# Keys and values of a token tile in three matmul groups instead of four, in a gated linear-attention kernel

## The chip, the cores and the metric

The kernel runs on one core of a Trainium2 chip. Time is device time in microseconds (us) of one execution, the median over several runs. The profile comes from one execution. Its engines are PE (TensorE, the matmuls), PEld (weight loads of TensorE), DVE (VectorE), ACT (ScalarE), POOL (GpSimd) and SP (SyncE, which issues most DMAs). "L92" is line 92 of the kernel.

## The reference

x has 2048 tokens of D = 576 columns, and all data are float32.

```python
xn = _layernorm(x)
# s: linear attention, 32 heads of 18 columns
q, k, v = heads of (xn @ wqkv)
pq, pk = q @ w_phi, k @ w_phi                        # per head
phi_q = concat(softmax(pq), softmax(-pq))            # per head, and phi_k from pk
kv = phi_k^T v;  z = sum of phi_k over tokens
s = ((phi_q kv) / (phi_q z + 1e-6)) @ wo
# g: a feed-forward layer of width 4608
g = silu((silu(xn @ w_gate) * (xn @ w_up)) @ w_down)
return x + s * g
```

## The kernel before

The work runs in four stages. The **preparation** (lines 137 to 254, about 0 to 71 us of the profile) normalizes the tokens, transposes them into the tiles X (`XB`), and lays out the weights. The **key/value loop** (lines 347 to 378, about 71 to 227 us) goes over 16 tiles of 128 tokens and sums phi_k^T v into `kvp`. The **query loop** (lines 431 to 496, to about 493 us) forms q, the numerators and the projection by `wo`. Then the **feed-forward** part runs to the end. Some of its matmuls are taken out as "early tiles" (line 110, tile `pe`), which have lower priority than the attention and fill TensorE where that has nothing ready.

Every float32 product is taken as a sum of products of rounded parts: operands are split into a high part (type fp32r) and a low part, and `xw` (line 82) adds up 14 matmuls for one output: for each half of the 576 rows, two chunks with three products each, and a 96-row chunk in which the parts are stacked. The tokens' tile is the stationary operand, and the weights stream past, so the number of columns of the output is the width of each matmul.

The weights of keys and values lie side by side in `KVWH` and `KVWL` (1152 columns): 576 for the keys, into which `w_phi` has been folded (`fold`, line 210, call at line 234), then 576 for the values, split from six loaded chunks at lines 242 to 249 by ACT, POOL and DVE. The six loads and the five of the query weights (line 252) share five buffers (`wst`).

In the key/value loop a token tile goes through these steps, in program order:

- lines 350 to 353: two groups of 14 matmuls of 288 columns for the keys, into the two PSUM banks of `pk` (tag `p2`, one buffer);
- lines 354 to 356, and `softmax_parts` (line 268): on DVE per head max, subtraction, min, subtraction, all four reading `pk`; two exponentials on ACT; then sum, reciprocal and multiplication on DVE, which give `phi`;
- lines 358 to 369: two groups of 14 matmuls of 288 columns for the values, each into a one-bank tile `pv` (tag `p`, one buffer), and copies of them on ACT into `v`, in which the 576 columns lie in five groups of seven heads (GW = 126 columns, the last 72) with a column of ones each;
- lines 370 to 371, between the two value groups: `kv_step` (line 286) of the tile before, ten matmuls of phi against v;
- lines 372 to 377: `background` (line 325), small steps that form sums of X for the feed-forward part on POOL, ACT and DVE (lines 305 to 323), and store them by DMA.

The order of instructions on each engine is fixed when the program is built: a planner takes instructions by priority (program order, raised where the code says `high_priority`) and by its own estimate of when their operands and buffers are ready. On the chip each engine follows its list and waits for semaphores. A tile with one buffer can be written again only when all readers of its last contents are done. PSUM has eight banks of 512 float32 columns; in the loop three hold `kvp`, two `pk`, one `pv`, and two the early tiles. In the profile both `p` and `p2` appear as `p`, since buffer numbers are left out.

Of the kernel before, what the change touches and what calls it, by code (L numbers as in the profile page):

```python
# [9 lines left out]
F32 = mybir.dt.float32  # L10
# [6 lines left out]
S, D, H, DH, F = 2048, 576, 32, 18, 4608  # L17
P = 128
# [5 lines left out]
HALF = D // 2  # L24
GH = 7
GW = GH * DH
# [11 lines left out]
def heads(ap):  # L38
    return ap.rearrange("p (h d) -> p h d", d=DH)


def spread(ap, n):
    return ap.unsqueeze(2).to_broadcast([P, n, DH])
# [3 lines left out]
def gated_hedgehog_kernel(ctx: ExitStack, tc, x, w_qk, w_v, w_phi, wo, w_gu, w_tail, w_down, ident_in, mask_in, out):  # L47
# [5 lines left out]
    nc = tc.nc  # L53
# [28 lines left out]
    def xw(ps, i, j, cols, wh, wl, stationary_x):  # L82
        pairs = []
        for k in range(2):
            b = XB[i][2 * j + k]
            for c in range(2):
                pairs += [(b[:, c, cols], w[:, k, c]) for w in (wh, wl)]
                pairs += [(b[:, 3 + c, cols], wh[:, k, c])]
            pairs += [(b[0:96, 2, cols], wh[0:96, k, 2])]
        for n, (a, b) in enumerate(pairs):  # L90
            l, r = (a, b) if stationary_x else (b, a)
            nc.tensor.matmul(ps, l, r, start=n == 0, stop=n == len(pairs) - 1)  # L92
# [30 lines left out]
    with ExitStack() as att:  # L123
# [8 lines left out]
        with ExitStack() as kst:  # L132
            kw = kst.enter_context(tc.tile_pool(name="kw", bufs=1))
            KVWH = kw.tile([P, 2, 3, 2 * D], F32R, name="KVWH")
            KVWL = kw.tile([P, 2, 2, 2 * D], F32R, name="KVWL")

            with ExitStack() as pst:
# [72 lines left out]
                def fold(ws, hi, lo):  # L210
                    for g, (o, w) in enumerate(GROUPS):
                        ps = pps.tile([P, 2, BT], F32, name="tp", bufs=3)
                        po = ps[:, :, 0:3 * P].rearrange("p a (c n) -> p a c n", c=3)
                        for k in range(2):
                            for c in range(3):
                                o2 = (3 * k + c) * P
                                nc.tensor.matmul(po[:, k, c, 0:w], ws[g][0:w, o2:o2 + P],
                                                 PHI[0:w, g].rearrange("p h f -> p (h f)")[:, 0:w],
                                                 start=True, stop=True)
                        split_rows(hi[:, :, :, o:o + w], lo[:, :, :, o:o + w], po[:, :, :, 0:w])  # L220
# [6 lines left out]
                wk = load_fold(0)  # L227
# [3 lines left out]
                first_weights = [early_weights(0)]  # L231
                with tc.issue_after(chain.ins):
                    norm_stats([3], xns[4:8])
                fold(wk, KVWH[:, :, :, 0:D], KVWL[:, :, :, 0:D])
                norm_block(3, xns[4:8])
                first_weights.append(early_weights(1))
                wv = []
# [3 lines left out]
                xns = load_x(0) + load_x(1)  # L241
                for n in range(6):
                    k, c = divmod(n, 3)
                    src, vh = wv[n][:, 0:D], KVWH[:, k, c, D:2 * D]
                    nc.scalar.copy(vh, src)
                    if c < 2:
                        nc.gpsimd.tensor_sub(KVWL[:, k, c, D:2 * D], src, vh)
                    else:
                        nc.vector.tensor_sub(vh[64:96], src[64:96], vh[64:96])
                wq = load_fold(1)  # L250
                norm_stats([0, 1], xns)
                norm_block(0, xns[0:4])
# [7 lines left out]
            kk = kst.enter_context(tc.tile_pool(name="kk", bufs=2))  # L260
            kps = kst.enter_context(tc.tile_pool(name="kps", bufs=1, space=PSUM))
# [5 lines left out]

            def softmax_parts(ps, e):
                m = kk_pool.tile([P, 2, H], F32, name="m")
                p4 = ps[:, :, 0:HALF].rearrange("p a (h d) -> p a h d", d=DH)  # L270
                for s, op in enumerate((ALU.max, ALU.min)):
                    m3 = m[:, s].rearrange("p (a h) -> p a h", a=2)
                    nc.vector.tensor_reduce(m3, p4, axis=AX.X, op=op)
                    nc.vector.tensor_sub(e[:, s * D:(s + 1) * D].rearrange("p (a h d) -> p a h d", a=2, d=DH), p4,  # L274
                                         m3.unsqueeze(3).to_broadcast([P, 2, H // 2, DH]))
                for s in range(2):
                    nc.scalar.activation(e[:, s * D:(s + 1) * D], e[:, s * D:(s + 1) * D], AF.Exp,
                                         scale=1.0 if s == 0 else -1.0)
                sm = kk_pool.tile([P, 2 * H], F32, name="sm")
                nc.vector.reduce_sum(sm, heads(e), axis=AX.X)  # L280
                nc.vector.reciprocal(sm, sm)
                return sm
# [3 lines left out]
            def kv_step(n, phi, v):  # L286
                for i in range(2 * NG):
                    g, s = divmod(i, 2)
                    o, w = GROUPS[g]
                    nc.tensor.matmul(kvp[i // 4][0:w, i % 4, 0:w + 1], phi[:, s * D + o:s * D + o + w], v[:, g, 0:w + 1],  # L290
                                     start=n == 0 and i % 4 == 0, stop=n == NT - 1, skip_group_check=True)
# [55 lines left out]
            pend = None  # L347
            for n in range(NT):
                i0, j0, cols = block((n + HT) % NT)
                pk = kps.tile([P, 2, 512], F32, name="p2")  # L350
                for i in range(2):
                    w = slice(i * HALF, (i + 1) * HALF)
                    xw(pk[:, i, 0:HALF], i0, j0, cols, KVWH[:, :, :, w], KVWL[:, :, :, w], True)
                phi = kk.tile([P, 2 * D], F32, name="phi", bufs=2)
                sm = softmax_parts(pk, phi)
                nc.vector.tensor_mul(heads(phi), heads(phi), spread(sm, 2 * H))
                v = vbuf[n % 2]
                for i in range(2):
                    w = slice(D + i * HALF, D + (i + 1) * HALF)
                    pv = kps.tile([P, 512], F32, name="p")  # L360
                    xw(pv[:, 0:HALF], i0, j0, cols, KVWH[:, :, :, w], KVWL[:, :, :, w], True)
                    a, m = (0, 2) if i == 0 else (3, 1)
                    o = a * GW - i * HALF
                    nc.scalar.copy(v[:, a:a + m, 0:GW], pv[:, o:o + m * GW].rearrange("p (g n) -> p g n", g=m))
                    if i == 0:
                        nc.scalar.copy(v[:, 2, 0:36], pv[:, 252:HALF])
                    else:
                        nc.scalar.copy(v[:, 2, 36:GW], pv[:, 0:90])
                        nc.scalar.copy(v[:, 4, 0:72], pv[:, 216:HALF])
                    if i == 0 and pend is not None:  # L370
                        kv_step(*pend)
                for _ in range(3):
                    next(background, None)
                if n == 6:
                    keep_x()
                pend = (n, phi, v)
                next(background, None)
# [4 lines left out]
            for i in range(3):  # L382
                for j in range(4 if i < 2 else 2):
                    w = GROUPS[(4 * i + j) // 2][1]
                    nc.scalar.copy(zc[0:w, 4 * i + j:4 * i + j + 1], kvp[i][0:w, j, w:w + 1])
            for a, m in ((0, 4), (4, 1)):
                o, w = GROUPS[a]
# [7 lines left out]
            for i in range(2 * NG):  # L395
                o, w = GROUPS[i // 2]
# [5 lines left out]
        with ExitStack() as qst:  # L402
# [28 lines left out]
            def q_tile(t):  # L431
                i0, j0, cols = block(t)
                pq = qps.tile([P, 2, 512], F32, name="p2")
                for i in range(2):
                    w = slice(i * HALF, (i + 1) * HALF)
                    xw(pq[:, i, 0:HALF], i0, j0, cols, QH[:, :, :, w], QL[:, :, :, w], True)
                e = qk.tile([P, 2 * D], F32, name="e", bufs=4)
                r = softmax_parts(pq, e)
                ez = qk.tile([P, 2 * D], F32, name="ez", bufs=1)
                nc.vector.tensor_mul(ez, e, zb)  # L440
                y = qk.tile([P, 2 * H], F32, name="y")
                nc.vector.reduce_sum(y, heads(ez), axis=AX.X)
                nc.vector.tensor_mul(y, y, r)
                den = qk.tile([P, H], F32, name="den")
                nc.vector.scalar_tensor_tensor(den, y[:, 0:H], DEN_EPS, y[:, H:], op0=ALU.add, op1=ALU.add)
                nc.vector.reciprocal(den, den)
                nc.vector.tensor_mul(r.rearrange("p (s h) -> p s h", s=2), r.rearrange("p (s h) -> p s h", s=2),
                                     den.unsqueeze(1).to_broadcast([P, 2, H]))
                last_e.append(nc.vector.tensor_mul(heads(e), heads(e), spread(r, 2 * H)))
                return e  # L450
# [419 lines left out]
    for i, n, f in units:  # L870
# [3 lines left out]
        if f >= EARLY:  # L874
            w = kept.pop() if i and kept else ready.pop(0)
# [4 lines left out]
        h = stored(h_dram[i, f], fill) if f < EARLY else gate_up(w, xo, fill, (i, f) == (0, EARLY))  # L880
        if n % 2 == 0:
            g = {"f": (f, units[units.index((i, n, f)) + 1][2]), "h": [h]}
# [58 lines left out]
```

## Time and profile before

| | |
|---|---|
| median of 3 runs | 1667.53 us (1667.0 to 1669.49) |
| profiled execution, span from first to last instruction | 1666.4 us |
| PE busy | 97% of the span |
| DVE busy | 73% |
| ACT busy | 43% |
| POOL busy | 38% |
| granted TensorE clock, mean | 0.997 |

No other time of the profiled execution is given; its span lies 1.1 us below the median of the runs. A line of the order of time gives the start in us, the duration, the engine, the line of the kernel, the operation, the output and inputs by tile name, shape and count, and in brackets the idle time before it with what ended it. Several equal instructions in a row are put into one line with a count. Matmuls overlap, so the distance between starts tells what one costs, and not its duration.

### The profile page before, as it was taken

Reading aid. Unit: us, or ns where it says so; the run is one execution under the profiler, and the core shown is the slowest. Engines: PE = TensorE matmul, PEld = TensorE weight load, DVE = VectorE, ACT = ScalarE, POOL = GpSimd, SP = SyncE. Lnnn points to the kernel's source line nnn. Section 1 sums busy time; section 2 is a strip of 40 time slices with the busy share of each in tenths; the row PEclk is TensorE's granted clock in tenths of the full one; section 3 lists DMA queues with packets and bytes.
Section 4 is the critical chain, followed back from the end, with each engine's and each line's share of the span. In section 5 each row is a group of like instructions: output and inputs, shape, how many; then the busy total and the mean of one; then the engine's idle time right before and its main releaser. Section 6 shows DMA issues by size and latency. Waiting matters only on the chain.

```text
span 1666.4 us, 25130 instructions
## 1 busy us (share of the span) xinstructions
PE 1621.8 (97%) x9441; PEld 1437.4 (86%) x9441; DVE 1218.2 (73%) x1722; ACT 718.3 (43%) x1389; POOL 632.7 (38%) x660
## 2 busy tenths in 40 slices
PE   6999999999999999999999999999999999999998
PEld 5899998999987778888888888888888888888887
DVE  7678759899842577888788788836667667667678
ACT  5533345444431455454544544445433333433334
POOL 3466500433101453554455464413234234133132
PEclk9999999999999999999999999999999999999999
DMA  8623313334227636445544544495444555555534
GB/s 285 211 77 112 105 40 105 112 121 118 63 82 273 214 134 205 155 164 171 195 156 169 189 165 160 156 336 165 147 140 136 165 182 186 170 178 183 144 114 170
DMA packets 118108, 264.68 MB, mean 159 GB/s; under 512 B 12419, under 2 KB 48387, under 8 KB 116195
## 3 DMA queue, kind: packets, MB, share of 16 engines
q1 hardware_dynamic: 107628, 247.44, 45.1%
q0 software_dynamic: 3072, 11.02, 2.4%
q10 hardware_dynamic: 7286, 4.63, 0.9%
q8 instruction: 74, 1.21, 0.3%
q14 instruction: 48, 0.39, 0.1%
HBM read 164.21 MB, written 98.83 MB: 158 GB/s over the span
## 4 chain that ended last, share of the span: by engine, by line
PE 54%; DVE 8%; issue 1%; DMA 1%; POOL 0%; ACT 0%; DVEq 0%; POOLq 0%; ACTq 0%; SPq 0%
PE px L570 20%; PE pd L669 19%; PE pw L570 10%; PE py L570 5%; DVE hh L59 2%; DVE dw L59 1%; DVE ha L630 1%; DVE hb L626 1%; DVE acc L794 1%; DVE s L604 1%; DVE w L59 1%; DVE X L794 0%; DVE acc L641 0%; DMA ld<-in_B_w_gu 0%; POOL ld L560 0%
## 5 line engine op out<-in xcount | busy, mean ns | idle before, releaser
L669 PEld LDWEIGHTS pd<-dw,hh 128*128 128x128 f32 x3048 | 431.9, 189 | 41.1 <-DVE dw L59 7.2
L669 PE MATMUL pd<-dw,hh 128*128 128x288 f32 x3048 | 450.3, 298 | 15.8 <-DVE dw L59 5.9
L570 PE MATMUL px<-X,w 128*128 128x512 f32 x1440 | 375.2, 395 | 0.3 <-ACT s L599 0.3
L570 PEld LDWEIGHTS px<-X,w 128*128 128x128 f32 x1440 | 262.5, 189 | 53.1 <-ACT s L599 5.2
L570 PE MATMUL pw<-X,w 128*128 128x512 f32 x720 | 188.0, 397 | 1.8 <-DVE s L604 1.8
L570 PEld LDWEIGHTS pw<-X,w 128*128 128x128 f32 x720 | 133.4, 189 | 35.6 <-DVE s L604 6.7
L604 DVE TENSOR_TENSOR s<-pw,s 128x512 f32<-128x512 f32 x120 | 82.7, 689 | 105.3 <-ACT s L599 94.2
L92 PE MATMUL pe<-X,wh 128*128 128x512 f32 (+1 forms) x480 | 152.1, 400 | 1.6 <-POOL X L199 0.6
L794 DVE TENSOR_TENSOR acc<-pd,acc 128x576 f32<-128x576 f32 x128 | 96.0, 752 | 63.9 <-PE pd L669 63.4
L599 ACT COPY s<-px 128x512 f32<-128x512 f32 x120 | 70.3, 585 | 156.0 <-PE px L570 156.0
L58 ACT CAST hh<-ha 128x512 fp32r<-128x512 f32 x140 | 83.1, 619 | 107.3 <-PE pd L669 72.2
L59 DVE TENSOR_TENSOR hh<-ha,hh 128x512 fp32r<-128x512 f32 x140 | 114.1, 840 | 18.1 <-ACT hh L58 17.6
L92 PE MATMUL p<-KVWH,X 128*128 128x288 f32 (+1 forms) x640 | 123.7, 298 | 1.2 <-DVE phi L274 1.2
L92 PEld LDWEIGHTS pe<-X,wh 128*128 128x128 f32 (+1 forms) x480 | 88.6, 189 | 19.5 <-DVE h L120 1.4
L766 POOL TENSOR_TENSOR hb<-hb 128x512 f32<-128x512 f32 x34 | 46.3, 1360 | 154.8 <-DVE hb L626 154.4
L92 PEld LDWEIGHTS p<-KVWH,X 128*128 128x128 f32 (+1 forms) x640 | 100.6, 189 | 1.9 <-issue 1.6
L59 DVE TENSOR_TENSOR w<-ld,w 128x512 fp32r<-128x512 f32 (+1 forms) x90 | 73.5, 817 | 32.8 <-ACT w L58 32.8
L570 PE MATMUL px<-X,wt 96*128 96x512 f32 x240 | 95.0, 396 | 0.0
L570 PE MATMUL py<-X,w 128*128 128x512 f32 x360 | 93.8, 394 | 0.7 <-ACT py L611 0.7
L779 POOL TENSOR_TENSOR ha<-ha 128x512 f32<-128x512 f32 x34 | 52.3, 1552 | 104.5 <-DVE hh L59 104.5
L58 ACT CAST w<-ld 128x512 fp32r<-128x512 f32 (+1 forms) x90 | 49.4, 549 | 96.9 <-POOL ld L560 61.8
L753 POOL TENSOR_TENSOR h<-ha,hb 128x512 f32<-128x512 f32 x34 | 46.7, 1373 | 116.9 <-DVE ha L630 99.9
(181 smaller groups left out, 3105.6 us busy)
## 6 DMA issues: line engine op xcount, KB each, us to landing
w_dram<-w SPq DMA_DIRECT2D x87, 512.0 KB, 3.0
w<-w_dram SPq DMA_DIRECT2D x87, 512.0 KB, 4.7
wt<-t_dram SPq DMA_DIRECT2D x59, 336.0 KB, 4.7
ld<-in_B_w_gu SPq DMA_DIRECT2D x30, 512.0 KB, 4.6
X<-sum_dram SPq DMA_DIRECT2D x8, 1280.0 KB, 6.7
rt<-in_B_w_down SPq DMA_DIRECT2D x33, 288.0 KB, 3.2
rb<-in_B_w_down SPq DMA_DIRECT2D x33, 288.0 KB, 3.0
w_dram<-w SPq DMA_DIRECT2D x29, 256.0 KB
```

Source lines behind the costliest of these rows:

```text
L58: nc.scalar.copy(hi, src)
L59: nc.vector.tensor_sub(lo, src, hi)
L92: nc.tensor.matmul(ps, l, r, start=n == 0, stop=n == len(pairs) - 1)
L570: nc.tensor.matmul(ps, l, r, start=first and n == 0, stop=last and n == len(mm) - 1, skip_group_check=True)
L599: nc.scalar.copy(t, ps)
L604: nc.vector.tensor_add(t, ps, t)
L626: nc.vector.tensor_mul(h[1], h[1], s3)
L669: nc.tensor.matmul(ps, l, r, start=first and n == 0 and m == 0, stop=n == len(hs) - 1 and m == 2, skip_group_check=True)
L753: sub(s, g["h"][0][0], g["h"][0][1])
L766: nc.gpsimd.tensor_add(a21, a21, g["h"][1][1])
L779: sub(a12, a12, g["h"][0][0])
L794: nc.vector.tensor_add(a2, pd[:, :, 0:HALF], a2)
```

## The change

Four groups of 288 columns become three, of 414, 414 and 324 columns. The first two hold 126 value columns beside one half of the keys each, the third holds the other 324 value columns. To make each group a contiguous slice, the columns of `KVWH` and `KVWL` are put in the order: values 0 to 125, keys, values 126 to 575. The six value chunks are therefore split in two pieces each, of 126 and 450 columns. `pk` is one tile of 1024 columns (two banks), in which the values stand at the outer ends (columns 0 to 125 and 800 to 925) and the keys between (126 to 413 and 512 to 799). ACT copies the values out of it with raised priority, one copy after each wide group and ahead of the softmax in program order. The KV step of the tile before comes after the third group. `softmax_parts` takes the sliced keys from its callers; for the queries that is the same as before.

```diff
-                fold(wk, KVWH[:, :, :, 0:D], KVWL[:, :, :, 0:D])
+                fold(wk, KVWH[:, :, :, GW:GW + D], KVWL[:, :, :, GW:GW + D])
...
-                    src, vh = wv[n][:, 0:D], KVWH[:, k, c, D:2 * D]
-                    nc.scalar.copy(vh, src)
-                    if c < 2:
-                        nc.gpsimd.tensor_sub(KVWL[:, k, c, D:2 * D], src, vh)
-                    else:
-                        nc.vector.tensor_sub(vh[64:96], src[64:96], vh[64:96])
+                    for a, b, o in ((0, GW, 0), (GW, D, GW + D)):
+                        src, col = wv[n][:, a:b], slice(o, o + b - a)
+                        vh = KVWH[:, k, c, col]
+                        nc.scalar.copy(vh, src)
+                        if c < 2:
+                            nc.gpsimd.tensor_sub(KVWL[:, k, c, col], src, vh)
+                        else:
+                            nc.vector.tensor_sub(vh[64:96], src[64:96], vh[64:96])
...
-                p4 = ps[:, :, 0:HALF].rearrange("p a (h d) -> p a h d", d=DH)
+                p4 = ps.rearrange("p a (h d) -> p a h d", d=DH)
...
-                pk = kps.tile([P, 2, 512], F32, name="p2")
-                for i in range(2):
-                    w = slice(i * HALF, (i + 1) * HALF)
-                    xw(pk[:, i, 0:HALF], i0, j0, cols, KVWH[:, :, :, w], KVWL[:, :, :, w], True)
-                phi = kk.tile([P, 2 * D], F32, name="phi", bufs=2)
-                sm = softmax_parts(pk, phi)
-                nc.vector.tensor_mul(heads(phi), heads(phi), spread(sm, 2 * H))
+                pk = kps.tile([P, 1024], F32, name="p2")
+                wide = HALF + GW
                 v = vbuf[n % 2]
                 for i in range(2):
-                    w = slice(D + i * HALF, D + (i + 1) * HALF)
-                    pv = kps.tile([P, 512], F32, name="p")
-                    xw(pv[:, 0:HALF], i0, j0, cols, KVWH[:, :, :, w], KVWL[:, :, :, w], True)
-                    a, m = (0, 2) if i == 0 else (3, 1)
-                    o = a * GW - i * HALF
-                    nc.scalar.copy(v[:, a:a + m, 0:GW], pv[:, o:o + m * GW].rearrange("p (g n) -> p g n", g=m))
-                    if i == 0:
-                        nc.scalar.copy(v[:, 2, 0:36], pv[:, 252:HALF])
-                    else:
-                        nc.scalar.copy(v[:, 2, 36:GW], pv[:, 0:90])
-                        nc.scalar.copy(v[:, 4, 0:72], pv[:, 216:HALF])
-                    if i == 0 and pend is not None:
-                        kv_step(*pend)
+                    w = slice(i * wide, (i + 1) * wide)
+                    xw(pk[:, 512 * i:512 * i + wide], i0, j0, cols, KVWH[:, :, :, w], KVWL[:, :, :, w], True)
+                    o = (512 + HALF) * i
+                    with tc.high_priority():
+                        nc.scalar.copy(v[:, i, 0:GW], pk[:, o:o + GW])
+                phi = kk.tile([P, 2 * D], F32, name="phi", bufs=2)
+                two = pk[:, GW:GW + 2 * (512 - GW)].rearrange("p (a n) -> p a n", a=2)
+                sm = softmax_parts(two[:, :, 0:HALF], phi)
+                nc.vector.tensor_mul(heads(phi), heads(phi), spread(sm, 2 * H))
+                pv = kps.tile([P, 512], F32, name="p")
+                w = slice(2 * wide, 2 * D)
+                xw(pv[:, 0:D - 2 * GW], i0, j0, cols, KVWH[:, :, :, w], KVWL[:, :, :, w], True)
+                nc.scalar.copy(v[:, 2:4, 0:GW], pv[:, 0:2 * GW].rearrange("p (g n) -> p g n", g=2))
+                nc.scalar.copy(v[:, 4, 0:72], pv[:, 2 * GW:D - 2 * GW])
+                if pend is not None:
+                    kv_step(*pend)
...
-                r = softmax_parts(pq, e)
+                r = softmax_parts(pq[:, :, 0:HALF], e)
```

## The prediction

> **What bounds the kernel now.** I read the profile from the outside in: the page for the engine that sets the end, the stretches for the stage that the change touches, the waits of that stage, and the order of time of one token tile. From the page:
>
> ```profile
> span 1666.4 us, 25130 instructions
> ...
> PE 1621.8 (97%) x9441; PEld 1437.4 (86%) x9441; DVE 1218.2 (73%) x1722; ACT 718.3 (43%) x1389; POOL 632.7 (38%) x660
> ...
> PE 54%; DVE 8%; issue 1%; DMA 1%; POOL 0%; ACT 0%; DVEq 0%; POOLq 0%; ACTq 0%; SPq 0%
> ```
>
> TensorE (PE) is busy for 97% of the span, so the kernel gets faster only where PE has less to do or waits less. The change touches the key/value loop, which runs from 71.5 to about 226.8 us; the view of stretches shows how PE fares in it, and the view of waits who holds it up.
>
> ```profile
> core 0: us, PE busy (x) PEld busy (x) DVE busy (x) ACT busy (x) POOL busy (x), PEclk, DMA share, GB/s
> 71.50:80.20 8.70, 7.47 (x51) 6.87 (x50) 3.28 (x9) 1.58 (x2) 5.97 (x8) 1.00 0.38 104
> 80.20:226.76 146.56, 146.56 (x1162) 146.06 (x1162) 112.01 (x125) 47.45 (x128) 80.28 (x76) 1.00 0.26 86
> ```
>
> ```profile
> PE p L92 <- DVE phi L274: 1.2, 1, 1.2
> ```
>
> After the first tile PE never stands still: 146.56 of 146.56 us. So the stage is worth what its matmuls take, plus any wait that the change brings in. VectorE (DVE) is at 112.01 of 146.56 us, three quarters; it has room, but not much for coming late.
>
> **What a tile's matmuls cost.** Durations of matmuls overlap, so I take the distance from start to start. Two places in the order of time, the down projection and the early feed-forward tiles:
>
> ```profile
> 1004.79 3.38 PE L669 MATMUL pd<-dw,hh 128*128 128x288 f32 x24
> 1008.01 1.55 PE L570 MATMUL px<-X,w 128*128 128x512 f32 x6
> 1009.39 0.40 PE L570 MATMUL px<-X,wt 96*128 96x512 f32 x1
> ```
>
> ```profile
> 504.52 0.40 PE L92 MATMUL pe<-X,wl 128*128 128x512 f32 x1
> ...
> 529.07 0.40 PE L92 MATMUL pe<-X,wl 128*128 128x512 f32 x1
> ```
>
> 24 matmuls of 288 columns take 1008.01 - 1004.79 = 3.22 us, 134.2 ns each. Six of 512 take 1.38 us, 230 ns. The two rows from line 92, the line of our loop, stand 15 rounds of 7 matmuls apart: 24.55 / 105 = 233.8 ns. A straight line through 288 and 512 columns has a slope of 0.445 ns a column and 6.2 ns that do not depend on the width (with the 230 ns: 0.428 and 11.0). The columns of a tile stay the same, 14 x 1152; only the number of matmuls falls, from 56 to 42. The saving is 14 x 6.2 = 87 ns a tile, **1.4 us** over 16 tiles. Its bounds are 0 (time proportional to columns, which the ratio 134.2/288 = 0.466 against 233.8/512 = 0.457 is not far from) and 2.5 us (11.0 ns). I take 1.4, since it comes from the same line and the same kind of operands. By the line, 414 columns take 190 ns and 324 take 150 ns.
>
> The Trainium skill, page "TensorE: Matmul & The Clock Gate", section "Back-to-back issue gap", gives the gap as the columns at 2.4 GHz plus about 2.5 ns. The trace agrees that the fixed part is small. By that figure the saving would be an estimated 14 x 2.5 ns x 16 = 0.6 us.
>
> **The wait that becomes tight.** The key tile (both halves, two banks, one buffer) may be overwritten by the next tile only when its readers are done. DVE reads it four times (max, subtract, min, subtract). One tile on DVE, and the same stretch on PE:
>
> ```profile
> 124.26 0.76 DVE L273 TENSOR_REDUCE m<-p 128x32 f32<-128x576 f32 x1 [1.80 <-PE p L92]
> 125.05 0.76 DVE L274 TENSOR_TENSOR phi<-p,m 128x576 f32<-128x576 f32 x1
> 125.72 0.75 DVE L273 TENSOR_REDUCE m<-p 128x32 f32<-128x576 f32 x1
> 126.51 0.76 DVE L274 TENSOR_TENSOR phi<-p,m 128x576 f32<-128x576 f32 x1
> ```
>
> ```profile
> 116.38 2.18 PE L290 MATMUL kvp<-v,phi 128*126 128x127 f32 x20
> 118.36 0.38 PE L92 MATMUL p<-KVWH,X 128*128 128x288 f32 x1
> ...
> 125.91 2.18 PE L290 MATMUL kvp<-v,phi 128*126 128x127 f32 x20
> ```
>
> The KV step takes 118.36 - 116.38 = 1.98 us, and 56 matmuls 7.55 us. The keys of this tile end where the 14 matmuls before 125.91 begin, at T0 = 125.91 - 14 x 0.1342 = 124.03. DVE begins 0.23 us later and is done at 127.27. Before the change PE has 14 value matmuls, the KV step and 14 more value matmuls to do after T0, 1.88 + 1.98 + 1.88 = 5.74 us, ahead of the next keys: DVE's 3.24 us are well covered. After it only the 324-column group and the KV step stand there: 14 x 0.150 + 1.98 = 4.08 us.
>
> And the chain grows. ScalarE (ACT) now copies value columns out of the same two banks first. What such a copy takes, and what DVE does when ACT reads its bank, stands in two other places:
>
> ```profile
> 111.00 0.26 ACT L364 COPY v<-p 128x126 f32<-128x126 f32 x1 [0.18 <-PE p L92]
> ```
>
> ```profile
> 227.85 0.35 ACT L385 COPY zc<-kvp 126x1 f32<-126x1 f32 x4 [1.96 <-PE kvp L290]
> 228.23 0.48 DVE L398 TENSOR_TENSOR km<-kvp,mask 126x126 f32<-126x126 f32 x2 [1.62 <-ACT zc L385]
> ```
>
> DVE's km needs nothing that zc makes; both only read kvp, and still DVE stood idle until ACT's read of that tile was over, and began 0.03 us after. So I put ACT's second copy into the chain: T0 + 0.23 (reaction) + 0.26 (copy) + 0.03, then DVE's 3.01 us, T0 + 3.53. PE's reaction is seen at the one wait of the stage:
>
> ```profile
> 79.24 0.76 DVE L274 TENSOR_TENSOR phi<-p,m 128x576 f32<-128x576 f32 x1
> ...
> 80.15 0.37 PE L92 MATMUL p<-KVWH,X 128*128 128x288 f32 x1 [1.23 <-DVE phi L274]
> ```
>
> DVE's subtraction there ended at 80.00, so 0.15 us. The next keys can start at T0 + 3.68, and PE comes at T0 + 4.08: **0.40 us of slack** in an ordinary tile, no wait. (Were the copy not ordered before DVE, 0.69.)
>
> The Trainium skill states why one would expect this order: page "PSUM — Partial Sum Buffer", section on bank collisions, says that two engines on one bank and quadrant at once are an error, reads against reads included. The trace agrees, with the 1.62 us that km waited. It is the rule that speaks against putting values beside keys.
>
> Not every tile is ordinary. The background sums put a DVE subtraction (line 320) between the last two reads in four tiles; the first and the last of them, and the longest insertion:
>
> ```profile
> 105.20 0.76 DVE L273 TENSOR_REDUCE m<-p 128x32 f32<-128x576 f32 x1 [0.54 <-PE p L92]
> ...
> 107.45 0.87 DVE L320 TENSOR_TENSOR shi<-sraw,shi 32x256 fp32r<-32x256 f32 x1
> 108.35 0.76 DVE L274 TENSOR_TENSOR phi<-p,m 128x576 f32<-128x576 f32 x1
> ...
> 136.03 1.40 DVE L320 TENSOR_TENSOR shi<-sraw,shi 32x256 fp32r<-32x256 f32 x1
> ...
> 190.94 0.76 DVE L273 TENSOR_REDUCE m<-p 128x32 f32<-128x576 f32 x1 [0.54 <-PE p L92]
> ...
> 194.09 0.76 DVE L274 TENSOR_TENSOR phi<-p,m 128x576 f32<-128x576 f32 x1
> ```
>
> There DVE's stretch is 108.35 + 0.76 - 105.20 = 3.91 us (3.91 again in the last), and 4.44 in the one with 1.40. The release comes at T0 + 4.58, a wait of 0.50 us three times, and at T0 + 5.11, 1.03 once: **+2.5 us**. The lower bound is 0, if early feed-forward matmuls, which the stage's last tile already uses as filler (row below), are put into those gaps, or the insertions fall elsewhere. I take the whole, since in the order of time no filler stands between 80.20 and 225 us now. Behind the waiting matmul stand, in PE's order, the rest of the tile; ACT's copies and DVE's next max wait for that, and nothing on SP or POOL does.
>
> **The other parts.** ACT's value copies go from five a tile to four, and the last two read the 324-column tile, needed again only a tile later: nothing. The first tile has no KV step, so its wait of 1.23 us stays about as it is (from -1.2, if filler covers it, to +0.4): 0. At the end, the last KV step waits for phi's division, and PE fills the time with early matmuls:
>
> ```profile
> 225.12 0.39 PE L92 MATMUL pe<-X,wl 128*128 128x512 f32 x1
> ...
> 226.76 2.19 PE L290 MATMUL kvp<-v,phi 128*126 128x127 f32 x20
> ```
>
> After the change 1.6 us more of filler is wanted there (5.74 - 4.08). These matmuls have to run some time; what is filled here is not paid after the attention: 0, or up to +1.6 if none is ready.
>
> In the preparation six casts of value weights, four subtractions on POOL and two on DVE become two each:
>
> ```profile
> 25.39 1.23 ACT L245 CAST KVWH<-wst 128x576 fp32r<-128x576 f32 x2
> ```
>
> ```profile
> 26.18 2.78 POOL L247 TENSOR_TENSOR KVWL<-wst,KVWH 128x576 fp32r<-128x576 f32 x2 [5.88 <-ACT KVWH L245]
> ```
>
> ```profile
> 52.30 2.78 PE L189 MATMUL tp<-ident,xn 128*128 128x128 f32 x24
> ```
>
> A piece more costs at most a whole small copy (0.26 us above), 6 x 0.26 = 1.6 us on ACT, less elsewhere. PE runs early matmuls until its transposes at 52.30 and starts them without a wait, so little shows: **+0.3**, between 0 and 1.6. The query weights' loads, behind these buffers in SP's queue, are as well covered.
>
> **Sum:** -1.4 + 2.5 + 0.3 = **+1.4 us**, on the profile's span 1667.8. The span is 1.1 us under the median of the runs, 1667.53, so **1668.9**.
>
> **Rivals.** (a) The four waits are covered by filler or vanish: -1.4 + 0.3, 1666.4. For it: filler exists. Against: none was used in 145 us. (b) Better than that: the full 2.5 us, and the first tile's wait filled, 1.2: 1663.8. Against: it takes the slope from another line. (c) Slower, paced by the chain: ACT's copy could stand behind one of the background casts:
>
> ```profile
> 109.39 0.83 ACT L319 CAST shi<-sraw 128x768 fp32r<-128x768 f32 x1 [1.57 <-DMA sum_dram<-shi]
> ```
>
> Or DVE could come late from the division before. If the release is 0.7 us later in every tile by this, it passes the point from which it decides, the 0.40 us of slack. Ten ordinary tiles then wait 0.3 us and four 0.7 more: 3.0 + 2.5 + 2.8 + 0.3 - 1.4 = +7.2, 1674.7. For it: DVE reaches the keys of some tiles hardly in time already (idle of only 0.54 us at 105.20). Against: ACT is a third busy, 47.45 of 146.56 us.
>
> **Chances.** Forecast (1667.5 to 1671) 0.40, (a) 0.25, (b) 0.10, (c) 0.25. The range from 1665 to 1675 leaves out (b) and the far end of (c). A measurement of this kernel can tell about 0.2%, 3.3 us: faster than 1664.2 is (b), 0.10; slower than 1670.9 is (c) and the forecast's edge, 0.28; within, 0.62. The likeliest case's own range is 1667.5 to 1671.
>
> **What would show it.** In the changed profile: starts of 414-column matmuls 190 ns apart and of 324 150 ns; DVE's max released by ACT's copy, not PE; waits of PE for phi (line 274) four times, 2.5 us in sum, and none in ordinary tiles. Wrong would be: a fixed cost above 11 ns a matmul, waits in nearly every tile, filler with its Silu table loads inside the loop, or a shift of more than 2 us outside 71 to 236 us.

## The result, and the profile after

| | before | after |
|---|---|---|
| median of six runs | 1667.03 us (1664.61 to 1669.49) | 1673.72 us (1670.7 to 1677.1) |
| profiled execution, span | 1666.4 us | 1670.7 us (its time 1672.52 us) |
| ratio after to before | | 1.0044, 95% interval 1.0034 to 1.0054 |

The change costs time: 0.44%, and the whole interval lies above the 0.2% that can be told from no change. The forecast was 1668.9 us in a range of 1665 to 1675; the range holds the time, the likeliest case (1667.5 to 1671) does not. A loss was forecast, of 1.4 us; 6.7 were measured. The profiled execution is a quick one, 1.2 us under its median, so the two traces show 4.3 us of the difference.

The page of after, the lines that answer to those shown of before:

```profile
span 1670.7 us, 24708 instructions
...
PE 1623.8 (97%) x9217; PEld 1433.0 (86%) x9217; DVE 1214.3 (73%) x1724; ACT 723.2 (43%) x1381; POOL 639.9 (38%) x664
...
PE 55%; DVE 7%; issue 1%; DMA 1%; ACT 0%; POOL 0%; DVEq 0%; ACTq 0%; POOLq 0%; SPq 0%
```

224 matmuls fewer (16 tiles by 14, 9441 to 9217), and PE is busy 2 us longer. So the page shows no saving, but not why. The view of stretches finds the place. First row: from the first key/value matmul to the last KV step. Second row: from there to the last early feed-forward matmul. After, then before:

```profile
core 0: us, PE busy (x) PEld busy (x) DVE busy (x) ACT busy (x) POOL busy (x), PEclk, DMA share, GB/s
72.05:236.85 164.80, 161.83 (x1008) 154.64 (x1008) 112.72 (x134) 52.11 (x115) 86.86 (x82) 1.00 0.25 82
236.85:544.55 307.70, 304.28 (x1897) 270.83 (x1895) 229.44 (x364) 132.65 (x237) 75.67 (x139) 1.00 0.38 123
```

```profile
71.51:226.76 155.25, 154.02 (x1212) 152.91 (x1211) 115.29 (x133) 49.03 (x129) 86.25 (x82) 1.00 0.26 87
226.76:539.36 312.60, 309.88 (x1918) 274.92 (x1918) 229.64 (x364) 130.93 (x237) 72.68 (x139) 1.00 0.38 121
```

The loop grew by 9.55 us and the stretch behind it shrank by 4.90. Most of that is early feed-forward work that moved: its matmuls have 512 columns and can be counted, 14 in the loop before and 35 after. At 0.234 us each (the pitch from the prediction) that is 4.9 us that only changed its place. Without them, "net" from here on, the loop went from 151.97 to 156.61 us, **+4.6**, and the stretch behind it from 184.13 to 184.14. The loop starts 0.5 us later, and the time behind the last early matmul is about 0.8 us shorter. The loss is in the loop.

Tile by tile (distance between the starts of KV steps): before, 14 times 9.53 us. After, ten ordinary tiles of 9.61 to 9.74, mean 9.67, and four with background subtractions, of 10.42, 10.50, 10.49 and 10.89, each with one early matmul inside. Ten times 0.14 is 1.4 us; the four are 3.2 us longer without their early matmuls. Together that is the 4.6; the first tile and the loop's end cancel. (The last of the ten also holds two early matmuls, in the place of three others that it lacks.)

From the view of waits, from 60 to 250 us, after (engine, line, who ended the wait: us in total, times, longest):

```profile
ACT v L360 <- PE p L92: 73.3, 31, 3.1
DVE m L275 <- ACT v L360: 34.1, 16, 3.2
...
PEld p L92 <- ACT v L360: 4.7, 16, 1.4
...
PEld p L92 <- ACT v L368: 3.1, 4, 1.1
...
PE p L92 <- DVE phi L276: 1.5, 3, 0.8
...
PE p L92 <- ACT v L360: 1.2, 1, 1.2
```

The second row is as forecast: in all 16 tiles DVE's max is released by ACT's copy. The third was in no step of the forecast: 16 times PE's weight load waits for ACT's copy. An ordinary tile in order of time shows where:

```profile
99.55 2.18 PE L292 MATMUL kvp<-v,phi 128*126 128x127 f32 x20
99.75 0.27 ACT L360 COPY v<-p 128x126 f32<-128x126 f32 x1 [2.99 <-PE p L92]
100.05 0.76 DVE L275 TENSOR_REDUCE m<-p 128x32 f32<-128x576 f32 x1 [2.18 <-ACT v L360]
...
102.30 0.76 DVE L276 TENSOR_TENSOR phi<-p,m 128x576 f32<-128x576 f32 x1
...
103.47 0.34 PE L92 MATMUL p<-KVWL,X 128*128 128x414 f32 x1
...
106.06 0.31 PE L92 MATMUL p<-KVWL,X 128*128 128x324 f32 x1
106.17 0.27 ACT L360 COPY v<-p 128x126 f32<-128x126 f32 x1 [2.02 <-PE p L92]
106.21 0.74 PE L92 MATMUL p<-KVWH,X 128*128 128x324 f32 x2
...
109.21 2.18 PE L292 MATMUL kvp<-v,phi 128*126 128x127 f32 x20
```

And on the weight load of the same place:

```profile
106.48 0.19 PEld L92 LDWEIGHTS p<-KVWH,X 128*128 128x128 f32 x1 [0.23 <-ACT v L360]
```

Read it from 103.47, the second matmul of the first wide group. The group has 14 of 0.188 us and is done at 105.91. Then come **three matmuls of the third group** (the row of 106.06 is the second of them; by the order of the matmuls from the first tile on, the third groups run one tile ahead), and only then the second wide group. It writes the other bank, but of the same tile that ACT has been reading since 106.17, and its weight load waits until that copy ends at 106.44. PE shows no idle time for this. The row of 106.21 joins the last of the three and the first matmul of the second wide group; unhindered they would take 0.150 + 0.34 = 0.49 us, and 0.74 is shown. The stop sits inside a "busy" duration, and that is why PE's busy time went up.

The three matmuls were put there by the order that the planner drew up, evidently to fill this wait: in late_copies below, which has no copy there, none stand there. They are missing behind T0 (99.55): the cover of DVE's chain is 1.98 + 11 x 0.150 = 3.63 us, not 4.08. DVE is done at 103.06, and with 0.15 us of reaction the wide tile is free at 103.21; PE arrives at 99.55 + 3.63 = 103.18 and goes on without a visible wait. The 0.40 us of slack are used up.

In a background tile it isn't enough:

```profile
109.47 0.27 ACT L360 COPY v<-p 128x126 f32<-128x126 f32 x1 [3.04 <-PE p L92]
109.76 0.76 DVE L275 TENSOR_REDUCE m<-p 128x32 f32<-128x576 f32 x1 [1.85 <-ACT v L360]
...
112.01 0.67 DVE L322 TENSOR_TENSOR shi<-sraw,shi 32x256 fp32r<-32x256 f32 x1
...
112.71 0.76 DVE L276 TENSOR_TENSOR phi<-p,m 128x576 f32<-128x576 f32 x1
...
112.92 0.40 PE L92 MATMUL pe<-X,wl 128*128 128x512 f32 x1
...
113.62 0.42 PE L92 MATMUL p<-KVWH,X 128*128 128x414 f32 x1 [0.29 <-ACT v L368]
```

DVE's last read ends at 113.47; from 109.21 that is 4.26 us against 3.63 of cover. One early matmul is drawn in, and PE still stands until 113.62. The name in the bracket (ACT's copy L368) is the profile's guess; the end that fits is DVE's, 0.15 us earlier. PE's waits in the other three background tiles are the row of 1.5 us in the view above.

The first tile has its wait as before, from another cause: its ACT copy, which writes `v`, came only after a store of the preparation (`x_dram<-xr`) was done. The likely reason is that `v` takes over memory of `xr`.

```profile
76.65 0.26 ACT L360 COPY v<-p 128x126 f32<-128x126 f32 x1 [4.70 <-DMA x_dram<-xr]
...
76.97 0.45 PE L92 MATMUL p<-KVWH,X 128*128 128x414 f32 x1 [1.16 <-ACT v L360]
```

### The profile page after: what moved, and what is told of

Its sections match the earlier page's. It is cut to its first block, busy times and chain, and to the rows that moved or that the text cites. A ratio compares the mean times of both kernels' runs of the same rounds, so it can differ in the third digit from the quotient of the medians.

```text
span 1670.7 us, 24708 instructions
## 1 busy us (share of the span) xinstructions
PE 1623.8 (97%) x9217; PEld 1433.0 (86%) x9217; DVE 1214.3 (73%) x1724; ACT 723.2 (43%) x1381; POOL 639.9 (38%) x664
## 4 chain that ended last, share of the span: by engine, by line
PE 55%; DVE 7%; issue 1%; DMA 1%; ACT 0%; POOL 0%; DVEq 0%; ACTq 0%; POOLq 0%; SPq 0%
PE px L570 20%; PE pd L669 19%; PE pw L570 10%; PE py L570 5%; DVE hh L59 2%; DVE ha L630 1%; DVE dw L59 1%; DVE acc L794 1%; DVE hb L626 1%; DVE w L59 1%; DVE s L604 0%; DVE acc L641 0%; DVE X L794 0%; DMA ld<-in_B_w_gu 0%; POOL ld L560 0%
## 5 line engine op out<-in xcount | busy, mean ns | idle before, releaser
L570 PE MATMUL pw<-X,w 128*128 128x512 f32 x720 | 188.0, 396 | 0.9 <-DVE s L604 0.9
L92 PE MATMUL p<-KVWH,X 128*128 128x414 f32 (+3 forms) x480 | 123.4, 345 | 3.0 <-DVE phi L276 1.5
L92 PEld LDWEIGHTS p<-KVWH,X 128*128 128x128 f32 (+1 forms) x480 | 87.5, 188 | 9.1 <-ACT v L360 4.7
```

Source lines behind the costliest of these rows:

```text
L570: nc.tensor.matmul(ps, l, r, start=first and n == 0, stop=last and n == len(mm) - 1, skip_group_check=True)
```

## The experiments

The theory, A: ACT and DVE sharing the wide tile costs the time, at two places. (i) The copy between the two wide groups holds the second one and takes three matmuls out of the cover. (ii) In four tiles the chain of copy and reads is late, by the background's cast on ACT ahead of it and its subtraction on DVE within it. (The trace of after has only the subtraction: apart from the first tile, every copy starts within 0.26 us of the end of its group.) The rival, B: the loss lies outside (the split casts of the preparation, or what follows the loop). The expectations also name C and C2: any second reader of the wide banks costs as much, wherever its copies stand. "Ordinary" and "background" are tile lengths in us. "Loop" and "behind" (the stretch after the loop) are net. "Idle" is PE's idle time behind the loop. "Half clock" is an estimate of what TensorE lost behind the loop at half the granted clock: half of its busy time there. Both are explained under "Where it goes".

| kernel | ratio to before, 95% interval | ordinary | background | loop | behind | idle | half clock |
|---|---|---|---|---|---|---|---|
| before | 1 | 9.53 | 9.53 | 151.97 | 184.1 | 2.7 | 0 |
| after | 1.0044 (1.0034 to 1.0054) | 9.67 | 10.42 to 10.89 | 156.61 | 184.1 | 3.4 | 0 |
| split_casts_only | 0.9995 (0.9986 to 1.0004) | 9.53 | 9.53 | 151.56 | 185.1 | 3.6 | 0 |
| late_copies | 1.0026 (1.0016 to 1.0035) | 9.43 | 10.13 to 10.57 | 152.94 | 187.0 | 4.9 | 1.7 |
| sums_on_pool | 1.0037 (1.0023 to 1.0050) | 9.61 to 9.72 | same | 156.02 | 188.3 | 6.0 | 1.7 |
| late_and_pool | 1.0021 (1.0011 to 1.0030) | 9.43 | 9.79 to 11.11 | 152.88 | 185.3 | 3.0 | 1.7 |
| dve_values | 1.0039 (1.0026 to 1.0051) | 9.43 | 10.25 to 11.98 | 155.41 | 185.6 | 4.3 | 0 |
| copies_elsewhere | 0.9970 (0.9959 to 0.9981) | 9.43 | 9.43 | 148.95 | 182.7 | 1.7 | 0 |
| dve_values_pool | 1.0003 (0.9994 to 1.0012) | 9.43 | 9.43 | 148.91 | 186.5 | 3.9 | 1.7 |
| late_all_pool | 0.9997 (0.9988 to 1.0005) | 9.43 | 9.43 | 148.96 | 184.8 | 2.7 | 1.5 |
| late_all_wo | 1.0011 (1.0002 to 1.0020) | 9.43 | 9.43 | 148.96 | 188.0 | 6.3 | 1.7 |
| before_all_wo | 1.0011 (1.0002 to 1.0020) | 9.53 | 9.53 | 151.64 | 185.0 | 4.5 | 0 |

**One part alone: the casts.** The kernel before, with the value weights cast in two pieces:

```
-src, vh = wv[n][:, 0:D], KVWH[:, k, c, D:2 * D]
+for a, b in ((0, GW), (GW, D)):
+    src, col = wv[n][:, a:b], slice(D + a, D + b)
```

> The kernel before, with each of the six value chunks split in two pieces of 126 and 450 columns in the preparation, and nothing else. Theory A2 and the prediction's +0.3 us: ratio 1.000 to 1.0005. Theory B (what is left of the loss comes from the preparation): 1.001 to 1.003.

0.9995: the preparation costs nothing, and this form of B is out.

**Both copies behind both wide groups**, so that nothing stands between the groups:

```
     xw(pk[:, 512 * i:512 * i + wide], ...)
+for i in range(2):
     o = (512 + HALF) * i
```

> Both value copies out of the wide tile come after both wide groups, instead of one after each. Theory A (the loss lies in the loop, and its root is that the second wide group waits for ACT's copy out of the first, which also draws matmuls of the third group ahead and so shortens the cover of DVE's reads): the ordinary tile falls from 9.67 to about 9.42 us, the first tile's wait of 1.2 us goes, the four tiles with a background subtraction keep a wait of about 0.65 us each; in all about 2 us over the kernel before, ratio 1.001. Theory B (the loss lies outside the loop, in the split casts of the preparation and the reordered early tiles): ratio stays near 1.0044. Theory C (the loss is that ACT and DVE read the same banks in turn, wherever the copies stand): DVE starts even later than in the changed kernel, ratio 1.004 or more.

The order of time of late_copies:

```profile
98.31 2.18 PE L292 MATMUL kvp<-v,phi 128*126 128x127 f32 x20
...
105.90 0.43 ACT L361 COPY v<-p 128x126 f32<-128x126 f32 x2 [4.24 <-PE p L92]
106.37 0.76 DVE L275 TENSOR_REDUCE m<-p 128x32 f32<-128x576 f32 x1 [1.28 <-ACT v L361]
...
107.74 2.18 PE L292 MATMUL kvp<-v,phi 128*126 128x127 f32 x20
...
108.28 1.28 POOL L323 TENSOR_TENSOR sraw<-sraw,shi 128x512 f32<-128x512 f32 x1
108.61 1.22 DVE L322 TENSOR_TENSOR shi<-sraw,shi 32x256 fp32r<-32x256 f32 x1
...
110.77 0.42 PE L92 MATMUL p<-KVWH,X 128*128 128x414 f32 x1 [0.85 <-DVE phi L276]
```

The ordinary tile takes 107.74 - 98.31 = 9.43 us: part (i) is shown, 0.24 us a tile. The price of 42 matmuls can now be seen bare, 0.10 us under 56. The four background tiles still wait, here 0.85 us behind DVE's reads, with a subtraction of 1.22 us among them. The loop is 3.7 us shorter than after's, the whole 0.0018 of the time, 3.0 us. Theory C is out for ordinary tiles: DVE begins 0.2 us later after its keys than in after, and the tile is shorter all the same. The ratio of 1.0026 misses A's 1.001; the loop is only 1.0 us over before, and the rest lies behind it (187.0 against 184.1).

The subtraction is long because of POOL: it begins while POOL's row of 108.28 runs, and ends at 109.83, 0.27 us after it. The last section has the count.

**The background's subtraction on POOL**, alone and with the late copies:

```
-tc.keep_in_program_order(nc.vector.tensor_sub(hi[32:64, :, 2], r[32:64, j, 2], hi[32:64, :, 2]))
+nc.gpsimd.tensor_sub(hi[32:64, :, 2], r[32:64, j, 2], hi[32:64, :, 2])
```

> The changed kernel with the background's two small subtractions per sum taken from DVE to POOL, so that none can stand between DVE's reads of the wide tile. Theory A: the four tiles of 10.4 to 10.9 us become ordinary ones of 9.67, the other waits stay; about 3 us less than the changed kernel, ratio 1.0025. Theory B: no change, 1.0044. Theory C: 1.003 to 1.0044.

> Both edits: copies after both wide groups, and the small subtractions on POOL. Theory A: all tiles at about 9.42 us, only the later start of the loop (0.7 us) stays: ratio 0.999 to 1.000. Theory B: 1.0044. Theory C: 1.003.

Alone, it makes the background tiles ordinary, but every tile keeps 0.1 to 0.2 us over before (9.61 to 9.72 against 9.53), and the loop gains only 0.6 net. That is because its first tile costs 2.1 us more than after's: PE waits 1.75 us for ACT's copy there, and then the granted clock is half for 3.41 us (from 77.34; matmuls of 414 columns start 0.346 us apart). Both ratios miss theory A's. With the late copies the background tiles should have been free; four of them aren't. The order of time of late_and_pool:

```profile
104.71 0.83 ACT L321 CAST shi<-sraw 128x768 fp32r<-128x768 f32 x1 [1.32 <-DMA sum_dram<-shi]
105.45 0.42 ACT L361 COPY v<-p 128x126 f32<-128x126 f32 x2
105.91 0.76 DVE L275 TENSOR_REDUCE m<-p 128x32 f32<-128x576 f32 x1 [2.55 <-ACT v L361]
...
106.47 2.18 PE L292 MATMUL kvp<-v,phi 128*126 128x127 f32 x20
```

ACT's copies start when the background's cast ends, at 105.45, with no idle time between. The third group ahead of the KV step takes 2.1 us, so the wide groups were done at 106.47 - 14 x 0.150 = 104.37, and with 0.2 us of reaction the copies could have begun at 104.6: they came 0.9 us late (2.0 and 2.2 in the two longest tiles). The cast itself had waited, by the bracket for the store of an earlier sum. This is the mechanism of rival (c), in four tiles and not in all, and not in after.

**DVE copies the values itself** after its reads, so that ACT doesn't touch the tile:

```
-nc.scalar.copy(v[:, i, 0:GW], pk[:, o:o + GW])
+nc.vector.tensor_copy(v[:, i, 0:GW], pk[:, o:o + GW])   # after the four reads
```

> DVE itself copies the 252 value columns out of the wide tile, after its four reads; ACT does not touch the wide banks. Theory A2 (ordinary tiles lose through the copy between the wide groups; tiles with background work lose because DVE's chain starts behind ACT's copies, which may stand in ACT's queue behind a background cast, and is stretched by the background subtraction): ordinary tiles 9.42 us, as with late copies; in the four background tiles only the inserted subtraction remains, about 0.4 us over; ratio 0.999 to 1.000. Theory C2 (any reader added to the wide tile costs as much, since it adds to the time until the tile is free): as with late copies, 1.0026.

A miss. Ordinary tiles are at 9.43, but three background tiles at 11.9 to 12.0:

```profile
108.50 1.29 DVE L323 TENSOR_TENSOR shi<-sraw,shi 32x256 fp32r<-32x256 f32 x1
109.82 0.76 DVE L276 TENSOR_TENSOR phi<-p,m 128x576 f32<-128x576 f32 x1
...
110.50 0.28 DVE L365 COPY v<-p 128x126 f32<-128x126 f32 x1
...
110.81 1.35 DVE L323 TENSOR_TENSOR shi<-sraw,shi 32x256 fp32r<-32x256 f32 x1
112.19 0.29 DVE L365 COPY v<-p 128x126 f32<-128x126 f32 x1
...
112.63 0.42 PE L92 MATMUL p<-KVWH,X 128*128 128x414 f32 x1 [1.78 <-DVE v L365]
```

Two subtractions, 2.64 us, lie between DVE's last uses of the tile, one of them between the two copies. Each of the two ended 0.28 us after a subtraction of POOL that was under way when it began. A longer chain on one engine gave the background more gaps to fall into.

**Both causes gone**, in three ways: no copies out of the wide banks at all (copies_elsewhere, which puts other columns in the place of the first 252 value columns, and so serves for its time only); DVE's copies with the subtractions on POOL; late copies on ACT with cast and subtraction on POOL.

```
-nc.scalar.copy(v[:, i, 0:GW], pk[:, o:o + GW])
+nc.scalar.copy(v[:, i, 0:GW], pv[:, i * GW:i * GW + GW])   # copies_elsewhere
```

```
-tc.keep_in_program_order(nc.scalar.copy(hi, r[:, j]))
+nc.gpsimd.tensor_copy(hi, r[:, j])                         # late_all_pool
```

> The value copies of the first 252 columns read the third group's tile instead of the wide tile (so those value columns are wrong, and the work of ACT is the same): no engine but DVE reads the wide banks. Theory A: no wait at the second wide group, DVE starts 0.3 us earlier than with the copies, no wait in any tile: ratio 0.999 to 1.000, about as both edits together. Theory B: 1.0044. Theory C: 0.999 to 1.000 here, while the kernel with late copies stays at 1.004.

> The same with the small background subtractions on POOL. Theory A2: every tile at 9.42 us, no wait in the loop, about 3 us less than the kernel before if nothing outside the loop moves: ratio 0.997 to 0.999. Theory C2: 1.002, as with late copies and POOL.

> Late copies on ACT, and the background's cast as well as its small subtraction on POOL, so that nothing of the background is left on ACT or DVE. Theory A2: all tiles at 9.42 us, since ACT's copies are never late; POOL is slower with the cast, but has a third of the loop idle: ratio 0.998 to 1.000. Theory C2: the chain is as long as with late copies, waits of 0.3 to 0.6 us remain: 1.002.

The loop of copies_elsewhere, then that of late_all_pool, in the view of stretches:

```profile
71.23:224.87 153.64, 153.64 (x994) 152.06 (x993) 112.09 (x133) 46.88 (x115) 85.80 (x82) 1.00 0.27 88
```

```profile
71.15:226.43 155.28, 155.28 (x1000) 153.46 (x1000) 104.57 (x117) 38.04 (x99) 114.13 (x114) 1.00 0.26 87
```

PE is busy in all of it. All three loops come to 148.9 us net, 3.0 below before: 1.6 to 1.8 for the matmuls and 1.2 for the first tile's wait, which filler now covers. So theory A is shown for the loop from both ends: with either cause left the tiles are longer, with neither they aren't. C2 is out as well: late_all_pool has ACT's copies and no wait. But the whole time follows only in copies_elsewhere. In the other two it is that of before (1.0003 and 0.9997), and the stretch behind the loop is longer, by 2.4 us in dve_values_pool and 0.7 in late_all_pool.

**Where it goes.** At the start of the query loop of late_all_pool DVE stood in order behind a subtraction that waits for ACT's cast of the output weights:

```profile
238.69 0.67 ACT L58 CAST WOH<-ez 126x576 fp32r<-126x576 f32 x1 [4.03 <-DMA tl<-in_B_w_tail]
...
239.39 0.87 DVE L59 TENSOR_TENSOR WOL<-ez,WOH 126x576 fp32r<-126x576 f32 x1 [4.48 <-DMA tl<-in_B_w_tail]
...
240.19 0.74 DVE L275 TENSOR_REDUCE m<-p 128x32 f32<-128x576 f32 x1
```

So the last pair moved that subtraction to POOL too, with the regrouping (late_all_wo) and without it (before_all_wo: four groups of 288, the same three moves):

```
-split(WOH[0:w, g], WOL[0:w, g], wr[0:w, 0:D])
+nc.scalar.copy(WOH[0:w, g], wr[0:w, 0:D])
+nc.gpsimd.tensor_sub(WOL[0:w, g], wr[0:w, 0:D], WOH[0:w, g])
```

> late_all_pool plus one more move: in the loop over five groups that loads the output weights, the subtraction that makes WOL goes from VectorE to GpSimd, so that VectorE's softmax reads of the first query tile stand behind no wait for ScalarE's WOH cast (in late_all_pool that cast began at 238.69 after 4.03 us behind the transfer of tl, VectorE's subtraction at 239.39, and TensorE then waited 1.57 and more for VectorE's e). Theory A (the loop's gain of 3.0 us is lost at this handover): tiles 9.43 again, the loop full, and the stretch from the last kv step to the first tile's end 1 to 3 us shorter than in late_all_pool's 184.8 net, 1663 to 1665.5, ratio 0.998 to 0.999. Theory B (the handover isn't what eats it; the planner lays the query loop out anew and the time moves elsewhere): within 1 us of late_all_pool's 1666.05, ratio 0.9992 to 1.0003. GpSimd's slower subtraction could also make the first use of WOL late, after the first query tiles: then above 1.0005.

> The kernel before (four groups of 288 columns) with the same three moves to GpSimd as late_all_wo: the background cast, the background's small subtraction, and WOL's. Beside late_all_wo it shows what the regrouping itself is worth once nothing on ScalarE or VectorE is late. Theory A: tiles 9.53 and the first tile's 1.23 us wait stay, so it is 2 to 3.5 us above late_all_wo, 1665 to 1668, ratio 0.999 to 1.0005. Theory B (what follows the loop decides and the regrouping is worth nothing at the end): within 1 us of late_all_wo.

Loop and the stretch behind it, late_all_wo and then before_all_wo:

```profile
71.76:227.04 155.28, 155.28 (x1000) 153.45 (x1000) 104.42 (x117) 38.06 (x99) 114.19 (x114) 1.00 0.26 87
227.04:540.51 313.47, 307.14 (x1905) 273.44 (x1905) 225.18 (x359) 127.08 (x233) 81.10 (x144) 0.99 0.38 121
```

```profile
72.30:227.21 154.91, 154.01 (x1211) 152.91 (x1211) 102.96 (x117) 37.04 (x113) 113.75 (x114) 1.00 0.26 88
227.21:540.65 313.44, 308.96 (x1918) 274.61 (x1917) 226.79 (x359) 128.53 (x235) 79.73 (x144) 1.00 0.38 121
```

The explanation by this one handover fails: without that subtraction in DVE's order the stretch behind the loop is no shorter, and none of PE's long waits there names `WOL`. Both kernels have the same ratio, 1.0011, with medians of 1667.9 and 1667.44 us. The loop with the regrouping is 2.7 us shorter net (155.28 - 27 x 0.234 against 154.91 - 14 x 0.234), the stretch behind it 3.1 us longer. Of these, 1.9 us are PE standing (313.47 - 307.14 = 6.33 against 4.48). The granted clock accounts for the rest: its mean behind the loop is 0.99 in late_all_wo. Two pieces of that run, in the view of stretches:

```profile
269.11:272.53 3.42, 1.32 (x7) 0.83 (x6) 3.42 (x7) 0.83 (x1) 0.00 (x0) 1.00 0.00 0
272.53:275.94 3.41, 3.41 (x9) 2.65 (x9) 3.37 (x7) 0.00 (x0) 0.00 (x0) 0.50 0.41 99
```

PE stood for 2.1 us up to 272.10, while DVE was busy without a break. In the next 3.41 us PE was busy throughout, at half the clock, which by an estimate costs 1.7 us, half of that time. The twelve traces hold 24 stretches of 3.41 or 6.83 us at half clock between the loop's start and 1640 us. Each begins right after 3.41 us in which PE was busy for 3% to 51%; of the other pieces of 3.41 us only one had PE busy as little as that.

This accounts for most of the differences behind the loop. Six kernels have one such stretch there, and before and after have none. "Behind" varies from 182.7 to 188.3 us over these kernels, though only one pair edits anything in it; less "idle" and "half clock" it is 180.0 to 181.5 in all twelve. It also accounts for copies_elsewhere, whose trace is 4.8 us shorter than that of late_all_pool and 5.2 us shorter than that of dve_values_pool, with the same loop: the half-clock stretches behind the loop and in the feed-forward part cost the other two 4.6 and 3.2 us more, and PE's idle time behind the loop 1.0 and 2.2 us.

Two things stay open. Why one kernel has these waits and another has not is settled only so far that the planner lays out the query loop anew for each. And each trace is one execution: the feed-forward part, edited in none, varies from 1124.2 to 1127.8 us between them, and the half-clock stretches don't explain that. Even undisturbed in its loop, the regrouping gave nothing that can be measured.

## Why the prediction was right and wrong

- **PE bounds the loop; a wait added there is paid in full.** Right. 4.6 us were added in the loop, and the stretch behind it gave nothing back.
- **Matmuls, -1.4 us.** Right, a little small: 0.10 us a tile against 0.087, 1.6 us over 16 tiles, seen in the kernels without waits. The prediction's other estimate, 0.6 us, is too small here; the measurement decides.
- **Ordinary tile, 0.40 us of slack.** This is the step that failed. It held that "only the 324-column group and the KV step stand there", 4.08 us. ACT's second copy was put into DVE's chain, rightly; the first copy, between the two wide groups, was taken as costing nothing. It holds the second group, evidently because both lie in one tile, and three matmuls moved in front of it. The forecast for ten tiles was -0.9 us; they brought +1.4. late_copies takes this alone away, and the tile falls to 9.43 us. The Trainium skill, page "PSUM — Partial Sum Buffer", section "PSUM bank collisions raise a hardware error", says that two engines on different banks run side by side. By it the chip did not ask for this wait; the trace shows only that it was kept, 16 times and 4.7 us. A tile of its own for each bank wasn't tried.
- **Four background tiles, +2.5 us.** The mechanism was right. The four brought 3.2 us where -0.3 + 2.5 was forecast: -0.4 for the cheaper matmuls, +1.0 for the wait at the second wide group, which these tiles have too, and +2.6 for DVE's chain. That 2.6 lies so near to 2.5 is partly luck: the cover was 0.45 us shorter than reckoned, 1.8 in sum, while one early matmul a tile filled 0.9 and the inserted subtractions were together 0.7 us shorter than before.
- **First tile and loop's end, 0.** Right: net of filler nothing changed. 14 early matmuls became 35 in the loop, work that only moved.
- **Preparation, +0.3.** Nothing in split_casts_only; within the bounds.
- **The rivals.** The outcome has the size of (c), 1674.7, but not its mechanism: in after no copy of ACT stood behind a background cast (that is seen only in late_and_pool, in four tiles), and the loss of the ordinary tiles has the other cause. That the range, drawn wide for (c), holds the time is luck. Two signs named as wrong did appear: a wait in nearly every tile, and early matmuls inside the loop. (a) and (b) did not come about, though the three kernels without the waits come near (b)'s loop (3.0 of its 3.7 us).

## What to carry to other kernels

When values of another reader are put into a buffer, go through every writer of that buffer, and not only the last release: a copy between two groups that share a tile held the second group here, though it wrote another bank. Reckon a cover from the order that will stand after the change, since what fills a new wait is taken out of the cover of another. And before fighting for 0.1 us a tile, ask whether the stage behind it will keep the gain: here 2.7 us were gone again within the next 314 us. Look at the granted clock of that stage too: where PE stood for about half of 3.41 us or longer, it lost about 1.7 us more afterwards.

## What the runs showed of the hardware

- A PE wait of a quarter of a microsecond hides in the busy column: the row of two matmuls shows 0.74 us instead of 0.49, with the wait only on the weight load (0.23 us). Distances between starts show it, busy shares don't.
- The DVE subtraction of 32x256 waits for POOL. It stands 96 times in the six kernels that keep it on DVE. In 47 of them POOL had nothing under way at its start, or at most 0.14 us of it left, and it took 0.41 to 0.42 us. The other 49 took 0.43 to 1.56 us, and every one ended 0.27 to 0.28 us after the POOL instruction that was under way at its start.
- The granted TensorE clock went to half for 3.41 us at a time (6.83 in three cases) right after 3.41 us in which PE was busy for about half of the time or less; matmuls of 414 columns then start 0.346 us apart instead of 0.188.
- POOL took over the background's cast and subtraction (114.13 us busy of 155.28 in late_all_pool) without PE standing once in the loop. The cast of 128x768 took 0.82 us there in the median, about as long as the 0.83 us on ACT.
